# Batch 0 of a linear-attention and feed-forward kernel: k's sums, denominators, division and turns in another order

## The chip, the cores and the metric

The kernel runs on one core of a Trainium2 chip. The core has five engines that run side by side, each through its own instructions in order: TensorE (PE in the profile; PEld is its loading of weights), VectorE (DVE), ScalarE (ACT), GpSimd (POOL) and SyncE (SP). They wait for one another by semaphores. Data comes from the chip's memory by DMA, which SyncE and GpSimd issue here. The metric is the device time of one execution in microseconds (us).

## The reference

```python
theta = np.pi / 2.0 * pos / S                      # S = 576 positions
phi(x) = concat([relu(x) * cos(theta), relu(x) * sin(theta)])   # 64 -> 128 features
q_p, k_p = phi(q), phi(k)                          # 8 batches, 8 heads
kv  = einsum('bhsf,bhsd->bhfd', k_p, v)
z   = sum(k_p, axis=2)                             # the sums of k
num = einsum('bhsf,bhfd->bhsd', q_p, kv)
den = einsum('bhsf,bhf->bhs', q_p, z)[..., None] + 1e-06
x   = (num / den) as [4608 tokens, 512]
h   = x @ w_in                                     # 512 x 2048
out = (h * sigmoid(1.702 * h)) @ w_out             # 2048 x 512
```

Inputs and output are float32; the kernel multiplies in bfloat16 and adds up in float32.

## The kernel before

Work goes batch by batch. Each batch has 576 tokens: four chunks of 128 (0 to 3) and a tail of 64 (chunk 4). The order of every engine's instructions is the order in which the program is written; nothing reorders it. A helper layer puts in the semaphore waits from the tiles that instructions read and write, and hands out buffers from pools: `pmm` has four one-bank PSUM tiles named `mm`, `pat` has two two-bank PSUM tiles named `at`.

For batch 0 nothing can hide the attention, so it stands alone at the start of the program (from `idle(22)`, line 377, to `start_block(0)`, line 416):

- SyncE loads k and then q in two pieces each. GpSimd waits for the first piece of k (the copy into `gate`, L137) and then issues v in two halves that are cast to bfloat16 on the way (`vb`, L139), then the three pieces of w_in, then the loads of batch 1: `load(kf, k, 1)` (line 419), two pieces of w_out, `load_q(1)` (line 422), v, two more pieces of w_out. A load waits until the steps that read its target tile before are done, and holds up what is behind it in GpSimd's queue.
- `idle` (L340) gives TensorE matmuls of zeros while k is on its way.
- `trig` (L151 on ScalarE, L153 on VectorE) makes one of nine steps j of relu times cosine or sine, 64 positions each and all heads, of k (into `kr`) or of q (into `qn0`).
- `kv_mm` (L214) multiplies k's features with a right-hand side, for head pair i, step j and each head of the pair in its own half of the partitions (64 rows), adding up over j. With a column of ones it gives k's sums z (column 64 of the `at` tile), later with `vb` the 64 columns of kv. `kv_evac` (L219) copies 65 columns a head to `kvs` in bfloat16.
- `qturn_pe` (L182) turns two steps of q (a chunk c) by TensorE, `qevac` (L190 on ScalarE, L192 on VectorE) copies the turned q into `qT`.
- `num_mm(c)` (L227) multiplies chunk c of qT with kvs: 64 numerators and one denominator a head. `num_div(c)` adds 1e-6 to the eight denominators (L235), takes reciprocals (L237) and multiplies (L239) into `xn`.
- `xturn_mm(c)` (L256) turns xn into the unused columns of the same `at` tile, `xturn_evac` (L263) copies it with ScalarE into `xT`, the left input of the feed-forward part.
- `start_block` (line 348): `mm1_part` (L279) makes the first four output blocks of x times w_in a chunk of tokens at a time, with the chunks' products and turns in between; `gelu` (L284) is ScalarE's activation into `g`; `mm1` is a whole block of 512 tokens.

Then come the other blocks of mm1, the tail's (L300), and `mm2` (L328), the product of g with w_out, whose result ScalarE copies (L332) and GpSimd stores (L335). Within mm2 of batch 0 stands the attention of batch 1 (lines 425 to 463: its k steps, q steps with DMA transposes, products, divisions and turns), the handover; the program then calls `start_block(1, opened=True)`. From there on batches repeat in a loop (line 466), with the next batch's attention hidden in the same way.

Of the kernel before, what the change touches and what calls it, by code (L numbers as in the profile page):

```python
# [19 lines left out]
def kernel(  # L20
# [64 lines left out]
    ones = const.tile([128, 2], BF16)  # L85
    nc.vector.memset(ones, 1.0)
# [59 lines left out]
    def trig(dst, src, j, act=False):  # L146
        i = src[:, :, ts(j, 64)]
        for cs, w in enumerate((cosw, sinw)):
            o = dst[:, j, :, ts(cs, 64)]
            if act:  # L150
                nc.scalar.activation(o, i, AF.Relu, scale=w[:, j:j + 1])  # L151
            else:
                nc.vector.tensor_scalar(o, i, 0.0, w[:, j:j + 1], op0=MAX, op1=MUL)  # L153
# [45 lines left out]
    st = {}  # L199

    def kv_open(i0=0, i1=NI):
        t = pat.tile([128, 2, 512], F32, name="at")
        for i in range(i0, i1):
            st["kv", i] = t[:, :, ds((i - i0) * 65, 65)]
        st["ps", i0] = t[:, :, 0:(i1 - i0) * 65]
        if i0 == 0:
            st["kvs"] = small.tile([128, 2, NI, VW], BF16, name="kvs", bufs=2)
# [9 lines left out]
    def kv_evac(i0, i1):  # L217
        o = st["kvs"][:, :, i0:i1, 0:65]
        nc.vector.tensor_copy(o, st["ps", i0].rearrange("p hh (i e) -> p hh i e", e=65))  # L219

    nums = {}

# [8 lines left out]
    def num_div(c):  # L231
        ps = nums[c][0]
        pv = ps[:, :, 0:260].rearrange("p a (h e) -> p a h e", h=4)
        den = small.tile([128, 2, 4], F32, name="den")
        nc.vector.tensor_scalar(den, pv[:, :, :, 64], 1e-6, None, op0=ADD)  # L235
        inv = small.tile([128, 2, 4], F32, name="inv")
        nc.vector.reciprocal(inv, den)  # L237
        xn = small.tile([128, 2, 4, 64], BF16, name="xn", bufs=4)
        nc.vector.tensor_tensor(xn, pv[:, :, :, 0:64],  # L239
                                inv.unsqueeze(3).to_broadcast([128, 2, 4, 64]), op=MUL)  # L240
        nums[c].append(xn)
# [9 lines left out]
    def xturn_mm(c):  # L251
        ps, xn = nums[c]
        xv = xn.rearrange("p a h e -> p (a h e)")
        for kc in range(KC):
            o = ps[:, kc // 2, ds(264 + (kc % 2) * 64, 64)].bitcast(BF16)
            nc.tensor.transpose(o, xv[:, ts(kc, 128)], ident)  # L256

    def xturn_evac(b, c):
        ps = nums.pop(c)[0]
# [3 lines left out]
        nc.scalar.activation(o, i, AF.Copy)  # L263
# [84 lines left out]
    def start_block(b, opened=False):  # L348

        if not opened:  # L350
            xturn_mm(0)
            xturn_evac(b, 0)
            xturn_mm(1)
            xturn_evac(b, 1)
            num_mm(2)
            num_div(2)
# [20 lines left out]
    idle(22)  # L377
    for j in (0, 1):
        trig(kr, kf, j)
    for j in (2, 6, 7, 8):  # L380
        trig(kr, kf, j, act=True)
    for j in (3, 4, 5):
        trig(kr, kf, j)
    kv_open(0, 2)
    kv_open(2, 4)
    kv_mm(0, NI, lambda r, i, j: ones[r, 0:1], 64, 1)
    for j in (0, 1):
        trig(qn0, qf0, j)
    qturn_pe(0)
    for j in (2, 3):  # L390
        trig(qn0, qf0, j, act=True)
    qturn_pe(1)
    idle(3)
    for j in (4, 5):
        trig(qn0, qf0, j)
    qturn_pe(2)
    for j in (6, 7):
        trig(qn0, qf0, j, act=True)
    qevac(0)
    trig(qn0, qf0, 8)  # L400
    qevac(1, act=True)
    qevac(2, act=True)
    kv_mm(0, 2, vb_rhs, 0, 64)
    kv_evac(0, 2)
    kv_mm(2, 4, vb_rhs, 0, 64)
    kv_evac(2, 4)
    qturn_pe(3)
    qevac(3, act=True)
    num_mm(0)
    num_div(0)  # L410
    num_mm(1)
    num_div(1)
    qturn_pe(4)
    qevac(4)
    x_open(0)
    start_block(0)
# [11 lines left out]
    for fc in range(5, FC):  # L428
        mm1(0, fc)
# [17 lines left out]
    mm2(0, 3, 8, 12)  # L447
    num_mm(0)
# [4 lines left out]
    mm2(0, 0, 12, 16)  # L453
    mm2(0, 1, 12, 16)
    xturn_mm(0)
    xturn_evac(1, 0)
    mm2(0, 2, 12, 16)
# [5 lines left out]
    start_block(1, opened=True)  # L463
# [79 lines left out]
```

## Time and profile before

| what | value |
|---|---|
| median of 3 runs | 292.15 us (292.04 to 292.19) |
| the profiled execution's own time | 292.69 us |
| its span | 291.0 us |
| TensorE busy | 282.5 us, 97% |
| VectorE busy | 123.9 us, 43% |
| ScalarE busy | 128.6 us, 44% |
| chain that ended last: line 328 (mm2) and line 279 (mm1) | 43% and 36% of the span |
| chain: load of v's first batch | 3% |

The profile is of one execution; times in it count from the start of its span. A group line gives the source line, the engine, the operation, output and inputs, the shapes and how often it ran. A line of the view in order of time gives start, length, engine, line and operation, and in brackets how long the engine had been idle and who released it. The ends of matmuls are modelled: a record of TensorE runs on some 0.2 us after the next one could start, so starts are the better measure of its pace.

### The profile page before, as it was taken

Reading aid. Unit: us, or ns where it says so; the run is one execution under the profiler, and the core shown is the slowest. Engines: PE = TensorE matmul, PEld = TensorE weight load, DVE = VectorE, ACT = ScalarE, POOL = GpSimd, SP = SyncE. Lnnn points to the kernel's source line nnn. Section 1 sums busy time; section 2 is a strip of 40 time slices with the busy share of each in tenths; the row PEclk is TensorE's granted clock in tenths of the full one; section 3 lists DMA queues with packets and bytes.
Section 4 is the critical chain, followed back from the end, with each engine's and each line's share of the span. In section 5 each row is a group of like instructions: output and inputs, shape, how many; then the busy total and the mean of one; then the engine's idle time right before and its main releaser. Section 6 shows DMA issues by size and latency. Waiting matters only on the chain.

```text
span 291.0 us, 5997 instructions
## 1 busy us (share of the span) xinstructions
PE 282.5 (97%) x2427; PEld 157.7 (54%) x2461; DVE 123.9 (43%) x355; ACT 128.6 (44%) x224; POOL 52.9 (18%) x60
## 2 busy tenths in 40 slices
PE   8979999999999999999999999999999999999995
PEld 3775646857545555555545554555455545565444
DVE  4774514872369036912692259415950520000000
ACT  7948633673115621463046313641265116773111
POOL 6250002200216100610143013401150010000000
PEclk9999999999999999999999999999999999999999
DMA  7999998998999885999598948995760341000322
GB/s 247 244 221 288 345 174 207 366 240 208 380 192 201 251 298 136 151 242 335 145 155 225 355 128 151 188 345 159 153 147 0 79 112 38 1 0 8 86 88 72
DMA packets 73211, 53.54 MB, mean 184 GB/s; under 512 B 52608, under 2 KB 62592, under 8 KB 73184
## 3 DMA queue, kind: packets, MB, share of 16 engines
q1 hardware_dynamic: 67216, 37.24, 53.4%
q0 software_dynamic: 5968, 15.93, 20.3%
q8 instruction: 19, 0.31, 0.4%
q14 instruction: 8, 0.07, 0.1%
HBM read 36.70 MB, written 9.44 MB: 159 GB/s over the span
## 4 chain that ended last, share of the span: by engine, by line
PE 91%; DMA 4%; ACT 1%; DVE 1%; issue 1%; POOL 0%; ACTq 0%
PE mm L328 43%; PE mm L279 36%; PE mm L307 4%; PE at L227 3%; PE at L214 3%; DMA vb<-in_v_dram 3%; PE mm L300 2%; ACT g L284 1%; DMA kf<-in_k_dram 1%; PE at L256 1%; DVE xn L239 1%; POOL vb L139 0%; DVE inv L237 0%; PE mm L182 0%; DVE den L235 0%
## 5 line engine op out<-in xcount | busy, mean ns | idle before, releaser
L328 PE MATMUL mm<-w_out_sb,g 128*128 128x512 bf16 (+1 forms) x507 | 116.0, 373 | 1.2 <-issue 0.2
L279 PE MATMUL mm<-xT,w_in 128*128 128x512 bf16 (+1 forms) x598 | 112.7, 345 | 0.5
L284 ACT ACTIVATE g<-mm 128x512 bf16<-128x512 f32 x128 | 75.6, 598 | 32.0 <-PE mm L279 31.9
L279 PEld LDWEIGHTS <-w_in 128*128 128x128 bf16 x608 | 61.7, 113 | 49.1
L328 PEld LDWEIGHTS <-g 128*128 128x128 bf16 x528 | 48.8, 98 | 50.0
L335 POOL DMA_DIRECT2D out_dram<-ysb x34 | 42.0, 1236 | 174.9 <-ACT ysb L332 174.8
L332 ACT ACTIVATE ysb<-mm 128x512 f32<-128x512 f32 (+1 forms) x37 | 21.7, 586 | 115.8 <-PE mm L328 115.8
L219 DVE CAST kvs<-at 128x520 bf16<-128x520 f32 (+1 forms) x9 | 5.8, 642 | 55.7 <-PE at L214 55.7
L239 DVE TENSOR_TENSOR xn<-at,inv 128x512 bf16<-128x512 f32 x40 | 27.7, 692 | 2.0 <-DMA xT<-xn 0.7
L153 DVE TENSOR_SCALAR kr<-kf,cosw 128x256 bf16<-128x256 f32 x68 | 23.9, 352 | 9.5 <-DMA kf<-in_k_dram 9.5
L153 DVE TENSOR_SCALAR kr<-kf,sinw 128x256 bf16<-128x256 f32 x68 | 23.2, 341 | 0.0
L235 DVE TENSOR_SCALAR den<-at 128x8 f32<-128x8 f32 x40 | 6.6, 166 | 37.1 <-PE at L227 37.1
L227 PEld LDWEIGHTS <-qT 128*128 128x128 bf16 x320 | 14.5, 97 | 7.3
L166 DVE TENSOR_SCALAR qn<-qf,cosw 128x512 bf16<-128x512 f32 (+1 forms) x33 | 15.8, 479 | 3.4 <-DMA qf<-in_q_dram 3.4
L227 PE MATMUL at<-kvs,qT 128*128 128x65 bf16 x320 | 15.9, 193 | 0.0
L166 DVE TENSOR_SCALAR qn<-qf,sinw 128x512 bf16<-128x512 f32 (+1 forms) x33 | 15.8, 479 | 0.0
L328 PE MATMUL mm<-w_out_sb,gt 128*128 128x512 bf16 x62 | 13.9, 380 | 0.2 <-issue 0.2
L214 PEld LDWEIGHTS <-kr 64*128 64x128 bf16 x648 | 10.2, 94 | 3.7 <-issue 3.0
L307 PE MATMUL mm<-xt,w_in 128*128 128x384 bf16 x64 | 10.6, 326 | 0.0
L328 PEld LDWEIGHTS <-gt 128*128 128x128 bf16 x64 | 6.2, 98 | 7.3
L174 DVE CAST vt<-vf 128x2304 bf16<-128x2304 f32 (+1 forms) x7 | 8.9, 1266 | 0.7 <-DMA vf<-in_v_dram 0.7
L307 PEld LDWEIGHTS <-w_in 128*128 128x128 bf16 x64 | 7.2, 113 | 3.3
(57 smaller groups left out, 101.9 us busy)
## 6 DMA issues: line engine op xcount, KB each, us to landing
kf<-in_k_dram SPq DMA_DIRECT2D x6, 1152.0 KB, 9.6
vf<-in_v_dram SPq DMA_DIRECT2D x6, 1152.0 KB, 12.4
qf<-in_q_dram SPq DMA_DIRECT2D x6, 1024.0 KB, 7.2
out_dram<-ysb POOLq DMA_DIRECT2D x24, 256.0 KB, 2.9
w_out_sb<-in_moe_w_out_dram POOLq DMA_DIRECT2D x4, 512.0 KB, 17.4
out_dram<-ysb POOLq DMA_DIRECT2D x10, 128.0 KB, 7.5
kf<-in_k_dram POOLq DMA_DIRECT2D x1, 1152.0 KB, 12.2
vf<-in_v_dram POOLq DMA_DIRECT2D x1, 1152.0 KB, 20.1
```

The lines of the kernel that those rows point to most:

```text
L153: nc.vector.tensor_scalar(o, i, 0.0, w[:, j:j + 1], op0=MAX, op1=MUL)
L166: nc.vector.tensor_scalar(o, i, 0.0, sc, op0=MAX, op1=MUL)
L174: nc.vector.tensor_copy(o, i)
L214: nc.tensor.matmul(st["kv", i][:, hh, ds(col, n)], kr[r, j, i, :], rhs(r, i, j), start=(j == 0), stop=(j == NS - 1))
L227: nc.tensor.matmul(ps[:, h // 4, ds((h % 4) * 65, 65)], qT[:, h, ts(c, 128)], st["kvs"][:, hh, i, 0:65], start=True, stop=True)
L239: nc.vector.tensor_tensor(xn, pv[:, :, :, 0:64], inv.unsqueeze(3).to_broadcast([128, 2, 4, 64]), op=MUL)
L279: nc.tensor.matmul(hp[fc][:, t0:t1], wcol(kc, fc), x[b][:, kc, t0:t1], start=(kc == 0), stop=(kc == KC - 1))
L284: nc.scalar.activation(g, hp.pop(fc), AF.Gelu_apprx_sigmoid)
L307: nc.tensor.matmul(hps[:, 128:B * 64], wcol(kc, fc), xt[:, kc, 128:B * 64], start=(kc == 0), stop=(kc == KC - 1))
L328: nc.tensor.matmul(yp[b, t, c0][:, c0:c1], w, w_out_sb[:, fc, c0:c1], start=(fc == 0), stop=(fc == FC - 1))
L332: nc.scalar.activation(ysb[:, c0:c1], yp[b, t, c0][:, c0:c1], AF.Identity)
L335: eng.dma_start(out=dst[:, c0:c1], in_=ysb[p0:p0 + n, c0:c1])
```

## The change

In batch 0:

- k's sums come from a new function `ksum`, with both heads of a pair in one matmul: all 128 rows of k's features against a selector `sel` of two columns (ones for the upper half of the partitions in one column, for the lower half in the other). 36 matmuls take the place of 72. They go into an `mm` tile, and VectorE copies the eight sums into column 64 of `kvs`. The kv products then have 64 columns a head and no longer share a tile with the sums (`kv_open` and `kv_evac` get a width n).
- The denominators of chunks 0 and 1 come from a new function `den_mm` (eight matmuls of one column, qT against the sums), with the addition and the reciprocal in `inverse`, both ahead of the product with v. For the other chunks `num_div` calls `inverse` itself, as before.
- The division of chunks 0 and 1 is made in two halves of four heads (`halves=True`), and their turns and ScalarE's copies in halves of two turns (`xturn_halves`).
- q's chunks 0 to 3 are all turned ahead of the product with v; q's copies stand in another order, and q's last step (j=8) and chunk 4 (turn, product, division) move behind the first parts of mm1.
- One of k's eight ScalarE steps (cosine of j=6) goes to VectorE.
- The 22 idle matmuls of 512 columns become 94 of 64 columns and 6 of 512; the three later ones become two.
- mm1's blocks 5 and 6 are called inside batch 0's script, between chunk 4's steps; the loop after it starts at 7.

In the handover from batch 0 to batch 1, `mm2(0, 0, 12, 16)` moves ahead of the first two products, and `mm2(0, 2, 12, 16)` is cut into two pieces around the first turns. `start_block` loses the part for batch 0 and is now used for batch 1 alone.

```diff
@@ -82,8 +82,11 @@
     scale = math.pi / 2.0 / S
     halfpi = const.tile([128, 1], F32)
     nc.vector.memset(halfpi, math.pi / 2.0)
-    ones = const.tile([128, 2], BF16)
-    nc.vector.memset(ones, 1.0)
+
+    sel = const.tile([128, 2], BF16)
+    nc.vector.memset(sel, 0.0)
+    nc.vector.memset(sel[0:64, 0:1], 1.0)
+    nc.vector.memset(sel[64:128, 1:2], 1.0)
     nc.scalar.activation(sinw, pos_f, AF.Sin, scale=scale)
     nc.scalar.activation(cosw, pos_f, AF.Sin, scale=-scale, bias=halfpi)
     gl = const.tile([128, 1], F32)
@@ -144,10 +147,11 @@
 
 
     def trig(dst, src, j, act=False):
+
         i = src[:, :, ts(j, 64)]
         for cs, w in enumerate((cosw, sinw)):
             o = dst[:, j, :, ts(cs, 64)]
-            if act:
+            if act is True or (act == "sin" and cs == 1):
                 nc.scalar.activation(o, i, AF.Relu, scale=w[:, j:j + 1])
             else:
                 nc.vector.tensor_scalar(o, i, 0.0, w[:, j:j + 1], op0=MAX, op1=MUL)
@@ -198,11 +202,11 @@
 
     st = {}
 
-    def kv_open(i0=0, i1=NI):
+    def kv_open(i0=0, i1=NI, n=65):
         t = pat.tile([128, 2, 512], F32, name="at")
         for i in range(i0, i1):
-            st["kv", i] = t[:, :, ds((i - i0) * 65, 65)]
-        st["ps", i0] = t[:, :, 0:(i1 - i0) * 65]
+            st["kv", i] = t[:, :, ds((i - i0) * n, n)]
+        st["ps", i0] = t[:, :, 0:(i1 - i0) * n]
         if i0 == 0:
             st["kvs"] = small.tile([128, 2, NI, VW], BF16, name="kvs", bufs=2)
 
@@ -214,11 +218,38 @@
                     nc.tensor.matmul(st["kv", i][:, hh, ds(col, n)], kr[r, j, i, :], rhs(r, i, j),
                                      start=(j == 0), stop=(j == NS - 1))
 
-    def kv_evac(i0, i1):
-        o = st["kvs"][:, :, i0:i1, 0:65]
-        nc.vector.tensor_copy(o, st["ps", i0].rearrange("p hh (i e) -> p hh i e", e=65))
+    def kv_evac(i0, i1, n=65):
+        o = st["kvs"][:, :, i0:i1, 0:n]
+        nc.vector.tensor_copy(o, st["ps", i0].rearrange("p hh (i e) -> p hh i e", e=n))
+
+    def ksum():
+
+        t = pmm.tile([128, 512], F32, name="mm")
+        for i in range(NI):
+            for j in range(NS):
+                nc.tensor.matmul(t[:, ts(i, 2)], kr[:, j, i, :], sel,
+                                 start=(j == 0), stop=(j == NS - 1))
+        nc.vector.tensor_copy(st["kvs"][:, :, :, 64].rearrange("p hh i -> p i hh"),
+                              t[:, 0:8].rearrange("p (i hh) -> p i hh", hh=2))
 
     nums = {}
+
+    inv_of = {}
+
+    def inverse(c, sums):
+        den = small.tile([128, 2, 4], F32, name="den")
+        nc.vector.tensor_scalar(den, sums, 1e-6, None, op0=ADD)
+        inv_of[c] = small.tile([128, 2, 4], F32, name="inv")
+        nc.vector.reciprocal(inv_of[c], den)
+
+    def den_mm(c):
+
+        ps = pmm.tile([128, 512], F32, name="mm")
+        for h in range(H):
+            i, hh = divmod(h, 2)
+            nc.tensor.matmul(ps[:, h:h + 1], qT[:, h, ts(c, 128)], st["kvs"][:, hh, i, 64:65],
+                             start=True, stop=True)
+        return ps[:, 0:8].rearrange("p (a h) -> p a h", a=2)
 
     def num_mm(c):
         ps = pat.tile([128, 2, 512], F32, name="at")
@@ -228,16 +259,15 @@
                              st["kvs"][:, hh, i, 0:65], start=True, stop=True)
         nums[c] = [ps]
 
-    def num_div(c):
+    def num_div(c, halves=False):
         ps = nums[c][0]
         pv = ps[:, :, 0:260].rearrange("p a (h e) -> p a h e", h=4)
-        den = small.tile([128, 2, 4], F32, name="den")
-        nc.vector.tensor_scalar(den, pv[:, :, :, 64], 1e-6, None, op0=ADD)
-        inv = small.tile([128, 2, 4], F32, name="inv")
-        nc.vector.reciprocal(inv, den)
+        if c not in inv_of:
+            inverse(c, pv[:, :, :, 64])
+        inv = inv_of.pop(c).unsqueeze(3).to_broadcast([128, 2, 4, 64])
         xn = small.tile([128, 2, 4, 64], BF16, name="xn", bufs=4)
-        nc.vector.tensor_tensor(xn, pv[:, :, :, 0:64],
-                                inv.unsqueeze(3).to_broadcast([128, 2, 4, 64]), op=MUL)
+        for a in (slice(0, 1), slice(1, 2)) if halves else (slice(0, 2),):
+            nc.vector.tensor_tensor(xn[:, a], pv[:, a, :, 0:64], inv[:, a], op=MUL)
         nums[c].append(xn)
 
     x = {}
@@ -248,19 +278,26 @@
     def x_cols(b, c):
         return x[b][:, :, ts(c, 128)] if c < 4 else xt[:, :, ts(b, 64)]
 
-    def xturn_mm(c):
+    def xturn_mm(c, kcs=range(4)):
         ps, xn = nums[c]
         xv = xn.rearrange("p a h e -> p (a h e)")
-        for kc in range(KC):
+        for kc in kcs:
             o = ps[:, kc // 2, ds(264 + (kc % 2) * 64, 64)].bitcast(BF16)
             nc.tensor.transpose(o, xv[:, ts(kc, 128)], ident)
 
-    def xturn_evac(b, c):
-        ps = nums.pop(c)[0]
+    def xturn_evac(b, c, a0=0, a1=2):
+        ps = nums[c][0]
         n = 128 if c < 4 else 64
         i = ps[:, :, 264:392].bitcast(BF16).rearrange("p a (k t) -> p a k t", k=2)[:, :, :, 0:n]
         o = x_cols(b, c).rearrange("p (a k) t -> p a k t", a=2)
-        nc.scalar.activation(o, i, AF.Copy)
+        nc.scalar.activation(o[:, a0:a1], i[:, a0:a1], AF.Copy)
+        if a1 == 2:
+            nums.pop(c)
+
+    def xturn_halves(b, c):
+        for a in range(2):
+            xturn_mm(c, (2 * a, 2 * a + 1))
+            xturn_evac(b, c, a, a + 1)
 
     def xturn_dma(b, c):
         xn = nums.pop(c)[1]
@@ -345,15 +382,8 @@
     def vt_rhs(r, i, j):
         return vt[r, j, i, 0:65]
 
-    def start_block(b, opened=False):
-
-        if not opened:
-            xturn_mm(0)
-            xturn_evac(b, 0)
-            xturn_mm(1)
-            xturn_evac(b, 1)
-            num_mm(2)
-            num_div(2)
+    def start_block(b):
+
         for c in range(4):
             for fc in range(4):
                 mm1_part(b, fc, c * 128, c * 128 + 128)
@@ -374,46 +404,79 @@
         xturn_evac(b, 4)
 
 
-    idle(22)
+    idle(94, 64)
+    idle(6)
     for j in (0, 1):
         trig(kr, kf, j)
-    for j in (2, 6, 7, 8):
-        trig(kr, kf, j, act=True)
+    trig(kr, kf, 2, act=True)
     for j in (3, 4, 5):
         trig(kr, kf, j)
-    kv_open(0, 2)
-    kv_open(2, 4)
-    kv_mm(0, NI, lambda r, i, j: ones[r, 0:1], 64, 1)
+    trig(kr, kf, 6, act="sin")
+    for j in (7, 8):
+        trig(kr, kf, j, act=True)
+    kv_open(0, 2, 64)
+    kv_open(2, 4, 64)
     for j in (0, 1):
         trig(qn0, qf0, j)
-    qturn_pe(0)
     for j in (2, 3):
         trig(qn0, qf0, j, act=True)
+    ksum()
+    qturn_pe(0)
+    qevac(0)
     qturn_pe(1)
-    idle(3)
+    dens = [den_mm(0)]
+    idle(2)
     for j in (4, 5):
         trig(qn0, qf0, j)
-    qturn_pe(2)
     for j in (6, 7):
         trig(qn0, qf0, j, act=True)
-    qevac(0)
-    trig(qn0, qf0, 8)
-    qevac(1, act=True)
+    inverse(0, dens[0])
+    qevac(1)
+    qturn_pe(2)
     qevac(2, act=True)
-    kv_mm(0, 2, vb_rhs, 0, 64)
-    kv_evac(0, 2)
-    kv_mm(2, 4, vb_rhs, 0, 64)
-    kv_evac(2, 4)
     qturn_pe(3)
     qevac(3, act=True)
+    kv_mm(0, 2, vb_rhs, 0, 64)
+    kv_evac(0, 2, 64)
+    inverse(1, den_mm(1))
+    kv_mm(2, 4, vb_rhs, 0, 64)
+    kv_evac(2, 4, 64)
     num_mm(0)
-    num_div(0)
+    num_div(0, halves=True)
     num_mm(1)
-    num_div(1)
+    num_div(1, halves=True)
+    x_open(0)
+    xturn_halves(0, 0)
+    xturn_halves(0, 1)
+    num_mm(2)
+    num_div(2)
+
+    def x_part(c):
+        for fc in range(4):
+            mm1_part(0, fc, c * 128, c * 128 + 128)
+
+    x_part(0)
+    num_mm(3)
+    num_div(3)
+    xturn_mm(2)
+    xturn_evac(0, 2)
+    x_part(1)
+    xturn_mm(3)
+    xturn_evac(0, 3)
+    trig(qn0, qf0, 8)
+    x_part(2)
+    x_part(3)
+    for fc in range(4):
+        gelu(fc)
+    mm1(0, 4)
     qturn_pe(4)
     qevac(4)
-    x_open(0)
-    start_block(0)
+    mm1(0, 5)
+    num_mm(4)
+    num_div(4)
+    mm1(0, 6)
+    xturn_mm(4)
+    xturn_evac(0, 4)
 
 
     load(kf, k, 1)
@@ -425,7 +488,7 @@
     load_wout(3)
     for j in range(NS):
         trig(kr, kf, j)
-    for fc in range(5, FC):
+    for fc in range(7, FC):
         mm1(0, fc)
     mm1_tail_first(0, 0)
     mm1_tail_first(0, 1)
@@ -445,22 +508,23 @@
     kv_evac(0, 4)
     mm2(0, 2, 8, 12)
     mm2(0, 3, 8, 12)
+    mm2(0, 0, 12, 16)
     num_mm(0)
     num_div(0)
     num_mm(1)
     num_div(1)
     x_open(1)
-    mm2(0, 0, 12, 16)
     mm2(0, 1, 12, 16)
+    mm2(0, 2, 12, 14)
     xturn_mm(0)
     xturn_evac(1, 0)
-    mm2(0, 2, 12, 16)
+    mm2(0, 2, 14, 16)
     xturn_mm(1)
     xturn_evac(1, 1)
     num_mm(2)
     num_div(2)
     mm2(0, 3, 12, 16)
-    start_block(1, opened=True)
+    start_block(1)
 
 
     for b in range(1, B):
```

## The prediction

> **What bounds the kernel now.** I read the page first, then TensorE's waits, then the stretches by window, then the order of time from 8 to 24 us, and last the handover to batch 1 near 47 us.
>
> ```profile
> PE 282.5 (97%) x2427; PEld 157.7 (54%) x2461; DVE 123.9 (43%) x355; ACT 128.6 (44%) x224; POOL 52.9 (18%) x60
> ```
>
> TensorE is busy for 97% of the span, so only time in which it has nothing to do can be won. Where it waits, the view of its waits says:
>
> ```profile
> PE at L256 <- DVE xn L239: 1.4, 2, 0.8
> PE at L214 <- DMA vb<-in_v_dram: 0.4, 1, 0.4
> PE mm L328 <- issue: 0.3, 2, 0.2
> ```
>
> All of it but 0.3 us lies in batch 0's attention. The windows (TensorE's busy time is the first figure after the length; the last three are granted clock, DMA share, GB/s) put it between 12.4 and 17.1 us; after that TensorE is full, so a shift of the first x by some time shifts the end by as much:
>
> ```profile
> 12.40:14.00 1.60, 1.16 (x49) 1.05 (x45) 0.79 (x2) 1.28 (x2) 1.09 (x3) 1.00 1.23 207
> 14.00:17.10 3.10, 1.71 (x38) 1.36 (x36) 2.43 (x8) 1.62 (x3) 3.10 (x5) 1.00 1.23 207
> 17.10:23.20 6.10, 5.95 (x103) 5.35 (x101) 3.18 (x9) 3.55 (x7) 1.45 (x3) 1.00 1.11 265
> 23.20:43.50 20.30, 20.20 (x149) 10.90 (x148) 8.05 (x25) 12.29 (x21) 0.55 (x1) 1.00 1.15 262
> ```
>
> The chain in order of time (start, length, what):
>
> ```profile
> 11.12 0.69 DVE L192 COPY qT<-mm 128x1024 bf16<-128x1024 bf16 x1
> 11.72 0.35 DVE L153 TENSOR_SCALAR qn<-qf,cosw 128x256 bf16<-128x256 f32 x1
> ...
> 12.89 0.71 PE L214 MATMUL at<-vb,kr 64*128 64x64 bf16 x36 [0.44 <-DMA vb<-in_v_dram]
> ...
> 13.54 0.62 PE L182 MATMUL mm<-ident,qn 128*128 128x128 bf16 x8
> 13.64 0.43 DVE L219 CAST kvs<-at 128x260 bf16<-128x260 f32 x1 [0.71 <-PE at L214]
> ...
> 14.44 0.17 DVE L235 TENSOR_SCALAR den<-at 128x8 f32<-128x8 f32 x1 [0.37 <-PE at L227]
> ...
> 14.88 0.69 DVE L239 TENSOR_TENSOR xn<-at,inv 128x512 bf16<-128x512 f32 x1
> 15.49 0.15 DVE L235 TENSOR_SCALAR den<-at 128x8 f32<-128x8 f32 x1
> ...
> 15.63 0.40 PE L256 MATMUL at<-ident,xn 128*128 128x128 bf16 x4 [0.76 <-DVE xn L239]
> ...
> 16.06 0.60 ACT L263 ACTIVATE xT<-at 128x512 bf16<-128x512 bf16 x1 [0.85 <-PE at L256]
> ...
> 17.14 1.06 PE L279 MATMUL mm<-xT,w_in 128*128 128x128 bf16 x16
> ```
>
> The second half of v lands, TensorE multiplies, VectorE copies and divides, TensorE turns, ScalarE copies, and the first product with w_in starts at 17.14. Records of TensorE include a tail of some 0.2 us; from start to start, 8 turns take 0.46 (13.54 to 13.99), 4 turns 0.23, 8 products of 65 columns 0.24, 16 products of 128 columns 0.90, a half of kT v 0.65 (12.89 to 13.54).
>
> **The change part by part.** Times are on this trace's axis.
>
> Sums of k. VectorE now does one step of k more (its cos of j=6), so its last ends at 8.60 (7.99 + 0.26 + 0.35), where ScalarE ended at 8.67. 30 of the 36 new matmuls remain then. No row shows a full 128-row load with 2 columns: the old ones go at 14 ns (56 in 0.79), the 65-column products at 30. I take 28, twice the half-height load, so 0.84, done at 9.5; bounds 14 and 60 ns move it by -0.4 and +1.0, and only what passes 9.8 counts, so 0 to +0.7 us. The small copy of the sums runs beside the turns.
>
> q's turns. VectorE's four steps of chunk 0 end at 9.76; chunk 0's second half of turns starts at 9.81 and ends at 10.21 (0.40). The copy to qT (0.69) now stands **ahead** of steps j=4, 5 on VectorE, which before ran while q landed (10.07 to 11.21). They now run 10.84 to 11.99 (0.60 after the copy's start, as 11.12 to 11.72 shows, then 3 x 0.265 + 0.35). Behind them TensorE has half of chunk 2 (12.04 to 12.27) and chunk 3 (to 12.73), both now ahead of v in its queue. So kT v's first half starts at 12.73, not 11.75; the two chunks' denominators (8 one-column products, 0.24) follow, and the second half starts at 13.70, not 12.89: v is no longer what it waits for. **+0.81**. The reciprocals and chunk 1's copy on VectorE end by 13.04, beside this.
>
> Division and turns. From the second half's start to the copy of kvs is 0.75 and from the copy's end to VectorE's first look at the product 0.37, as before: 14.45, 14.88, 15.25. The den and reciprocal (0.44, from 14.44 to 14.88) are gone from the chain, for two chunks. The halves: 256 elements a division, which I price at 0.42 by the 0.43 of the 260-element copy (0.35 from one half of 0.69) with 0.35 from start to start. But the built program carries two waits that the diff does not show: the first half's turns wait for **both** divisions of their chunk, and the second half's turns wait until ScalarE has **copied out the first half**. So: divisions end at 16.02; turns 16.07 (two take 0.29 to their end); copy 16.39 to 16.82 (0.43, the row of 256 elements of xt); turns 16.87; copy 17.19 to 17.62; chunk 1's first half beside that, copy 17.52 to 17.95; its last turns 18.00 to 18.12; and behind them in TensorE's queue the third chunk's product (0.24) and x's first part: 18.36 instead of 17.14. **+1.22**, the 0.81 included.
>
> From there to x's last part. Before, 17.14 to 21.02 (3.88): two products of 65 columns, two sets of turns, three parts of 0.90, a wait of 0.25 for xn at 18.53. Now chunk 4's product is gone from it, the wait is nearly the same (0.24; xn is ready 1.38 after its product's last start, as 14.24 to 15.62 before): 3.65. **-0.23**.
>
> After it. Chunk 4's turn of q (0.23) and product (0.24) are now in TensorE's full stretch, where before the first filled an idle spot. Its x turns stand one mm1 (0.86) behind its product, and xn needs 1.38: a new wait of 0.52. **+0.99**. That mm1(5) and mm1(6) go ahead of the turns costs nothing itself; they are only taken out of the later loop.
>
> Handover. One mm2 group of four (0.86) moves ahead of the products, which leaves 0.86 + 0.43 + 0.23 + 0.43 = 1.95 between chunk 1's last product and its turns; xn of chunk 1 is ready 2.66 after the first product's start (46.45 to 49.06, + 0.05), and TensorE comes there at 0.48 + 1.95 = 2.43. **+0.23**; before there was none. Bounds 0 to 0.3.
>
> What else moves. q's last step (j=8) goes behind xn of chunk 3 on VectorE, to about 21. GpSimd's load of the next q waits for it, so it is issued near 21.5 instead of 15.58, and the next v and the last two loads of w_out are queued behind it. I take 0, since DMA share is above 1 in both windows from 17.1 to 43.5: the backlog of k, w_in and w_out covers the gap. The worst is the whole 5.9 us less the 2.0 by which TensorE is later and the 0.86 of the moved group, 3.0. The next batch's k steps start behind one more division (25.99 becomes some 26.9); their user is at 43.5. ScalarE has four copies of 0.43 for two of 0.60 and idles at L263 anyway.
>
> The idle matmuls. 22 wide ones took 7.10, the first eleven at 0.43. Narrow ones cost at least 1/8 of that, 53 ns, at most some 60 (twice the 30 of 65 columns), so 94 and 6 end near 7.5, ahead of k at 8.6: 0.
>
> Sum: 1.22 - 0.23 + 0.99 + 0.23 = **+2.21 us**. The profiled execution took 292.69 (span 291.0 and 1.69 around it), so 294.9; it stands 0.54 above the median 292.15, so **294.35** as a median.
>
> **The rivals.**
> A. The clock. TensorE ran its first 4.4 us at half pace and was granted 1.00 since, though busy only 1.71 of 3.10 us from 14.0 to 17.1. From 7.5 on it now gets mostly thin work. If full pace came one period later, sums and turns would run 0.8 longer: 295.1; if it fell again before 13.9, the 2.6 us of TensorE's work on the chain would double: 296.9. The quoted stretch, which kept 1.00, speaks against it. The Trainium skill (TensorE: Matmul & The Clock Gate, Parts 1 and 4) says that an idle window brings the half clock back and that transposes don't count as busy; by that rule this change runs the risk. The 14.0 to 17.1 row, full of transposes, shows no drop.
> B. The halves overlap after all, because the two added waits cost nothing. Then x starts at 17.14, and the sum is -0.23 + 0.99 + 0.23: 293.1. The waits in the program speak against it.
> C. Not slower: v stays what TensorE waits for, because q's side on VectorE is done by 12.9. It decides if kT v's second half starts by 12.9; together with B that takes 0.81 more: 292.3, no measurable change. Against it: VectorE's line of 9.76, 10.93, 11.99 has no gap to give.
> D. The late q load reaches the handover: up to 297.3.
>
> **How the numbers follow.** My forecast 0.77, of its own range 293.6 to 295.3 (the sums' +0.7, the handover's and divisions' bounds); A 0.07, B 0.07, C 0.05, D 0.04. From 293.0 to 296.2 it leaves out C and parts of A and D and the tails of the first, under 2 in 10. A measurement tells 0.2%, 0.58 us, from nothing: C is the same (0.05) or a little faster; a gain needs C and the later waits gone as well, 0.04; slower is the rest.
>
> **What would show it.** In the changed trace: kT v's second half starts 13.4 to 14 with VectorE's q steps ahead of it, not v's DMA; ScalarE's four half copies of xT alternate with pairs of turns, 0.8 apart; x's first part starts near 18.4; TensorE waits 0.5 for xn one mm1 after chunk 4's product, and 0.2 for it in the handover; from there both traces run in parallel, 2.2 apart. Wrong would be: v's DMA still named before kT v, pairs of turns back to back, or a granted clock under 1.00 after 6 us.

## The result and the profile after

The changed kernel takes 296.53 us in the median of six executions (294.87 to 297.26); before it was 292.14. The ratio is 1.0145, with a 95% interval of 1.0114 to 1.0177: slower. The prediction said slower, but 294.35, and its range ended at 296.2, so it was wrong by its size.

The spread is the first thing to read, since in these executions the kernel before spreads over 0.15 us and this one over 2.4. The six executions fall into three groups by the mean clock that TensorE was granted: 1.000 (294.87), 0.993 (295.81, 295.85), 0.987 to 0.988 (297.21 to 297.26). The median lies between the second group and the third, where no execution was. The profiled execution took 295.85 (span 294.1, mean clock 0.993) and belongs to the middle group. From the page of the changed kernel, the busy time of the engines and the clock in forty slices:

```profile
PE 286.5 (97%) x2518; PEld 162.3 (55%) x2518; DVE 124.6 (42%) x362; ACT 127.9 (43%) x224; POOL 52.1 (18%) x60
PEclk9979999999999999999999999999999999999999
```

The span is 3.1 us longer, and one slice, the third (14.7 to 22.1 us), has a lower clock. The windows of the same execution (length, busy time and count of each engine, then granted clock, DMA share, GB/s) put its ends on 16.85 and 20.27 us:

```profile
13.44:16.85 3.41, 2.04 (x66) 1.72 (x65) 2.54 (x8) 1.29 (x2) 2.37 (x4) 1.00 1.25 211
16.85:20.27 3.42, 2.89 (x33) 2.72 (x33) 1.06 (x3) 1.04 (x3) 0.00 (x0) 0.50 1.12 209
20.27:23.68 3.41, 3.30 (x62) 3.15 (x61) 1.58 (x5) 1.49 (x3) 0.82 (x1) 1.00 1.08 341
```

The half clock lasts 3.41 us. It lies on the last turns and the first products with w_in, which are work that nothing hides. It also begins a whole number of such lengths, three, behind the point where the trace's record of the full clock starts (6.62), which is why the windows here are cut in this way.

In order of time the changed kernel's chain reads (cuts marked by dots):

```profile
10.18 0.69 DVE L196 COPY qT<-mm 128x1024 bf16<-128x1024 bf16 x1 [0.39 <-PE mm L186]
10.79 0.34 DVE L157 TENSOR_SCALAR qn<-qf,cosw 128x256 bf16<-128x256 f32 x1
...
12.75 0.70 PE L218 MATMUL at<-vb,kr 64*128 64x64 bf16 x36
...
13.67 0.70 PE L218 MATMUL at<-vb,kr 64*128 64x64 bf16 x36
...
15.21 1.41 DVE L270 TENSOR_TENSOR xn<-at,inv 128x256 bf16<-128x256 f32 x4 [0.37 <-PE at L258]
...
16.02 0.27 PE L286 MATMUL at<-ident,xn 128*128 128x128 bf16 x2 [0.60 <-DVE xn L270]
...
16.32 0.38 ACT L293 ACTIVATE xT<-at 128x256 bf16<-128x256 bf16 x1 [1.98 <-DVE xn L270]
16.76 0.52 PE L286 MATMUL at<-ident,xn 128*128 128x128 bf16 x4 [0.47 <-ACT xT L293]
...
17.11 0.66 ACT L293 ACTIVATE xT<-at 128x256 bf16<-128x256 bf16 x2 [0.40 <-PE at L286]
17.82 0.37 PE L286 MATMUL at<-ident,xn 128*128 128x128 bf16 x2 [0.53 <-ACT xT L293]
...
18.44 1.90 PE L316 MATMUL mm<-xT,w_in 128*128 128x128 bf16 x16
```

v's load is named nowhere: q's steps j=4, 5 start 0.61 behind the start of the copy to qT, and the product with v comes when TensorE gets to it: v's second half had landed by 13.10, where GpSimd's copy that waits for it starts, and is first used at 13.67. The turns run in pairs, each held by ScalarE's copy of the pair before it. The sixteen first products take 1.90 instead of 1.06, because they run at half clock. The waits of TensorE in the changed kernel (total, times, longest) say the same, with new ones for the copies:

```profile
...
PE at L286 <- ACT xT L293: 1.0, 2, 0.5
PE at L286 <- DVE xn L270: 1.0, 2, 0.6
PE mm L230 <- DVE kr L157: 0.4, 2, 0.2
PE at L258 <- DVE kvs L223: 0.3, 1, 0.3
...
```

Where the 3.1 us between the two profiled executions lie follows from the starts of the same work in both traces. The first product with w_in: 17.14 and 18.44, +1.30. The tail products of batch 0: 32.67 and 35.61, +2.94. x's last parts in the handover: 54.04 and 57.19, +3.15. The tails at the end: 253.15 and 256.30, +3.15. So all of it arises in batch 0's attention and the handover, and the steady loop adds nothing.

### The profile page after: what moved, and what is told of

Same layout as the page of the kernel before. It is cut to its first block, busy times and chain, and to the rows that moved or that the text cites. A ratio compares the mean times of both kernels' runs of the same rounds, so it can differ in the third digit from the quotient of the medians.

```text
span 294.1 us, 6155 instructions
## 1 busy us (share of the span) xinstructions
PE 286.5 (97%) x2518; PEld 162.3 (55%) x2518; DVE 124.6 (42%) x362; ACT 127.9 (43%) x224; POOL 52.1 (18%) x60
## 4 chain that ended last, share of the span: by engine, by line
PE 93%; DVE 2%; DMA 2%; issue 1%; ACT 0%; SPq 0%; ACTq 0%
PE mm L365 42%; PE mm L316 37%; PE mm L344 4%; PE at L218 3%; PE at L258 3%; DMA qf<-in_q_dram 2%; PE mm L337 1%; DVE xn L270 1%; PE at L286 1%; PE mm L186 1%; DVE qn L157 0%; DVE inv L243 0%; ACT xT L293 0%; DVE qT L196 0%; PE mm L250 0%
## 5 line engine op out<-in xcount | busy, mean ns | idle before, releaser
L365 PE MATMUL mm<-w_out_sb,g 128*128 128x512 bf16 (+1 forms) x528 | 117.4, 372 | 0.0
L316 PE MATMUL mm<-xT,w_in 128*128 128x512 bf16 (+1 forms) x608 | 114.7, 348 | 0.0
L372 POOL DMA_DIRECT2D out_dram<-ysb x34 | 41.1, 1210 | 176.6 <-ACT ysb L369 176.5
L270 DVE TENSOR_TENSOR xn<-at,inv 128x512 bf16<-128x512 f32 (+1 forms) x42 | 27.7, 665 | 1.7 <-PE at L258 0.4
L218 PEld LDWEIGHTS <-kr 64*128 64x128 bf16 x576 | 9.1, 94 | 2.6 <-issue 2.5
```

Source lines behind the costliest of these rows:

```text
L218: nc.tensor.matmul(st["kv", i][:, hh, ds(col, n)], kr[r, j, i, :], rhs(r, i, j), start=(j == 0), stop=(j == NS - 1))
L270: nc.vector.tensor_tensor(xn[:, a], pv[:, a, :, 0:64], inv[:, a], op=MUL)
L316: nc.tensor.matmul(hp[fc][:, t0:t1], wcol(kc, fc), x[b][:, kc, t0:t1], start=(kc == 0), stop=(kc == KC - 1))
L365: nc.tensor.matmul(yp[b, t, c0][:, c0:c1], w, w_out_sb[:, fc, c0:c1], start=(fc == 0), stop=(fc == FC - 1))
L372: eng.dma_start(out=dst[:, c0:c1], in_=ysb[p0:p0 + n, c0:c1])
```

## The experiments

Each was timed beside the kernel before, in four groups on four chips; the changed kernel itself was timed in the first comparison alone and not beside its variants. Since a fall of TensorE's clock is a thing that some executions have and others don't, two numbers are given: the median of the executions without such a fall (mean clock 0.997 or more), with what it is above the kernel before of the same comparison, also without falls; and how many executions had one. The kernel before had one in 5 of its 69 executions in these comparisons. The changed kernel itself: 294.87, 2.73 above, with a fall in 5 of 6, 3 of them two (by the mean clock, which is as far below 1 again; no such execution was profiled).

| kernel | full clock | above before | falls | ratio, 95% interval |
|---|---|---|---|---|
| changed | 294.87 | 2.73 | 5 of 6 | 1.0145, 1.0114 to 1.0177 |
| changed, later stretch filled | 294.83 | 2.73 | 2 of 4 | 1.0102, 1.0069 to 1.0135 |
| changed, both stretches filled | 294.85 | 2.62 | 0 of 4 | 1.0089, 1.0074 to 1.0104 |
| changed, wide idle matmuls | 294.73 | 2.63 | 3 of 4 | 1.0139, 1.0076 to 1.0202 |
| changed, whole division and turns | 294.06 | 1.96 | 0 of 6 | 1.0058, 1.0040 to 1.0076 |
| ... and chunk 4's turns later | 293.54 | 1.31 | 2 of 4 | 1.0071, 1.0052 to 1.0091 |
| ... or q's chunk 3 behind v | 293.40 | 1.15 | 1 of 7 | 1.0043, 1.0026 to 1.0059 |
| ... or v later | 294.12 | 1.89 | 2 of 4 | 1.0083, 1.0062 to 1.0105 |
| changed, all of these undone | 292.73 | 0.60 | 0 of 12 | 1.0011, 0.9999 to 1.0024 |
| before, halved division and turns | 292.86 | 0.76 | 4 of 10 | 1.0040, 1.0021 to 1.0059 |
| before, new handover | 292.39 | 0.14 | 0 of 12 | 1.0001, 0.9989 to 1.0014 |
| before, v later | 292.32 | 0.09 | 1 of 10 | 1.0001, 0.9987 to 1.0015 |
| before, chunk 4's turns first | 291.84 | -0.41 | 1 of 12 | 0.9988, 0.9976 to 1.0000 |

The intervals are of all executions, falls included; a difference of 0.1 to 0.2 us between rows is not to be read, and the full-clock figure of the changed kernel is a single execution, that with wide idle matmuls too.

**The later thin stretch filled.** Theory 1 was that the clock fell because TensorE had too little to do between 14.3 and 17.1.

```diff
     def xturn_halves(b, c):
         for a in range(2):
+            idle((3, 2, 0, 3)[2 * c + a])
             xturn_mm(c, (2 * a, 2 * a + 1))
             xturn_evac(b, c, a, a + 1)
...
     def idle(n, cols=512):
+        if n == 0:
+            return
```

> The changed kernel with eight more idle matmuls of 512 columns where TensorE waits for batch 0's division and copies (three ahead of the first pair of turns, two ahead of the second, three ahead of the fourth: 0.65, 0.43 and 0.65 us of waits of 0.7, 0.6 and 0.8). Theory 1, the clock: what my sum of +2.2 us lacks is the half clock that begins near 17 us, because TensorE's work between 14.3 and 17.1 is too thin. Then the granted clock is 1.00 in every execution, the sixteen first products take 0.90 from start to start instead of 1.68, and the time is about 294.9 with little spread, 1.6 us less than the changed kernel's median of 296.5. Theory 2, the spread and the rest come from elsewhere (transfers, the late q load): time and spread stay, 294.9 to 297.3. Theory 3: idle matmuls only get in the way: slower than 296.5.

The four took 294.74 and 294.92 at clocks of 0.998 and 1.000, and 295.91 and 295.95 at 0.994. Two falls in one execution did not come again, but single ones did. In the profiled execution the fall is elsewhere now; its windows:

```profile
7.31:10.72 3.41, 2.16 (x48) 1.85 (x48) 3.11 (x10) 2.58 (x7) 0.28 (x1) 1.00 1.16 280
10.72:14.14 3.42, 2.91 (x33) 2.06 (x36) 1.97 (x7) 2.62 (x6) 0.90 (x3) 0.50 1.23 205
14.14:17.55 3.41, 3.07 (x101) 2.37 (x99) 2.20 (x8) 1.02 (x2) 1.81 (x3) 1.00 1.22 210
```

The filled stretch is kept at full clock, and the half clock follows another one: k's sums with their two columns, q's turns and the wait for the first copy to qT. The theory was half right, as there are two thin stretches. The filling itself costs nothing: the full-clock time is that of the changed kernel.

**Whole division and turns.**

```diff
-    num_div(0, halves=True)
+    num_div(0)
     num_mm(1)
-    num_div(1, halves=True)
+    num_div(1)
     x_open(0)
-    xturn_halves(0, 0)
-    xturn_halves(0, 1)
+    xturn_mm(0)
+    xturn_evac(0, 0)
+    xturn_mm(1)
+    xturn_evac(0, 1)
```

> The changed kernel with division, turns and copies of chunks 0 and 1 whole again, everything else as changed. Theory 1: the halves cost 1.1 us on the chain (copy of the first half between the two pairs of turns, twice), so the first product with w_in starts at 17.3 instead of 18.44, and since the thin stretch is that much shorter, the clock falls less often: 293.7 where it stays 1.00, 294.7 to 296 where it falls. Rival: the halves overlap well enough, and undoing them changes nothing at a clock of 1.00 (294.9).

294.06, with all six at a clock of 1.000. TensorE in order of time:

```profile
13.54 0.70 PE L218 MATMUL at<-vb,kr 64*128 64x64 bf16 x36
...
15.82 0.40 PE L286 MATMUL at<-ident,xn 128*128 128x128 bf16 x4 [0.54 <-DVE xn L270]
16.42 0.40 PE L286 MATMUL at<-ident,xn 128*128 128x128 bf16 x4 [0.20 <-DVE xn L270]
16.91 0.40 PE L258 MATMUL at<-kvs,qT 128*128 128x65 bf16 x8
17.14 1.06 PE L316 MATMUL mm<-xT,w_in 128*128 128x128 bf16 x16
```

From the second half of the product with v to the first product with w_in it is 3.60 us. So undoing the halves wins 0.8 at full clock, and with no fall in these six, 2.5 against the changed kernel's median. The falls are rarer without the halves and not gone: the three variants of this kernel below had them in 2 of 4, 2 of 4 and 1 of 7. The 1.1 that I expected at full clock was too much by 0.3, and the rival, that they overlap, is out.

**The wide idle matmuls of before.**

```diff
-    idle(94, 64)
-    idle(6)
+    idle(22)
```

> The changed kernel with the 22 wide idle matmuls of before in place of 94 narrow and 6 wide. Theory 1: the narrow ones are not what lets the clock fall at 17 us; k's sums start at the same 8.2 to 8.6, and the clock still falls near 17 us in most executions: 294.9 to 297.3 as with the change. Rival: the narrow ones leave the clock's governor with too little work, and with the wide ones the clock is 1.00 throughout: 294.9.

294.73, 295.93, 296.32 and 298.30, the last three with falls: no change that four executions can tell. In its profile the clock falls at 18.73, after a stretch from 15.32 in which TensorE was busy 1.70 of 3.41 us. So the narrow idle matmuls are not what brings the falls. The 298.30, by its clock (0.988) an execution with two falls, is 3.6 above the one without; in the changed kernel two cost 2.4.

**The halves alone, in the kernel before.**

```diff
...
-        nc.vector.tensor_tensor(xn, pv[:, :, :, 0:64],
-                                inv.unsqueeze(3).to_broadcast([128, 2, 4, 64]), op=MUL)
+        inv = inv.unsqueeze(3).to_broadcast([128, 2, 4, 64])
+        for a in (slice(0, 1), slice(1, 2)) if halves else (slice(0, 2),):
+            nc.vector.tensor_tensor(xn[:, a], pv[:, a, :, 0:64], inv[:, a], op=MUL)
...
-            xturn_mm(0)
-            xturn_evac(b, 0)
-            xturn_mm(1)
-            xturn_evac(b, 1)
+            xturn_halves(b, 0)
+            xturn_halves(b, 1)
...
-    num_div(0)
+    num_div(0, halves=True)
     num_mm(1)
-    num_div(1)
+    num_div(1, halves=True)
```

> The kernel before with the halved division, turns and copies of chunks 0 and 1 alone. Theory 1: the first product with w_in starts 0.8 us later (17.9 instead of 17.14), as the pairs of turns alternate with ScalarE's copies: 292.9 to 293.0 at full clock; the thin stretch from 14.5 grows to 3.4 us, so a fall of the clock, with 1 us or more on top, is possible here. Rival: the halves overlap, 291.8.

0.76 more at full clock (expected 0.8), and 4 of 10 executions at 0.994 with 294.1 to 294.4. One part of the change alone thus brings both effects: the longer chain, and the fall of the clock in four in ten where the kernel before has it in 5 of 69 (1 of 15 beside it). TensorE's order shows the same alternation as in the changed kernel:

```profile
15.08 0.27 PE L257 MATMUL at<-ident,xn 128*128 128x128 bf16 x2 [0.82 <-DVE xn L241]
15.83 0.63 PE L257 MATMUL at<-ident,xn 128*128 128x128 bf16 x4 [0.47 <-ACT xT L264]
16.93 0.27 PE L257 MATMUL at<-ident,xn 128*128 128x128 bf16 x2 [0.47 <-ACT xT L264]
```

**Both thin stretches filled.**

```diff
     idle(94, 64)
-    idle(6)
+    idle(9)
...
     qturn_pe(1)
+    idle(2)
     dens = [den_mm(0)]
...
         for a in range(2):
+            idle((3, 2, 0, 3)[2 * c + a])
```

> The changed kernel with idle matmuls in both thin stretches: those of the first filled kernel (14.3 to 18 us), and five more between 7.9 and 11.5, three behind the first idle matmuls and two ahead of chunk 0's denominators. Theory 1, the clock: with only the later stretch filled, the two falls of the clock (297.2) did not come again, but one fall did (295.9), and in the profile it began at 11.0, behind the stretch of two-column sums and turns. With both filled the clock is 1.000 in every execution and the time 294.7 to 295.0. Rival: the governor doesn't go by such gaps, and 295.9 stays in about half of the executions.

294.53, 294.78, 294.91 and 295.23, none with a fall. The windows of its profile, cut at the same length from where its record of the full clock starts (4.34):

```profile
7.75:11.17 3.42, 2.67 (x58) 2.27 (x60) 2.80 (x11) 2.26 (x7) 0.00 (x0) 1.00 1.18 259
11.17:14.58 3.41, 3.15 (x95) 2.20 (x93) 2.52 (x10) 3.41 (x6) 1.29 (x3) 1.00 1.23 205
14.58:17.99 3.41, 3.02 (x48) 1.82 (x41) 1.97 (x6) 0.96 (x4) 1.43 (x3) 1.00 1.21 212
```

Same chain, 13 more idle matmuls, 1.7 us less in the median. Four executions are few, but the changed kernel went without a fall in one of six, and two other variants on the same chip fell in 2 of 4 each.

**Chunk 4's turns one block later** (on the kernel with whole division and turns).

```diff
     mm1(0, 6)
+    mm1(0, 7)
     xturn_mm(4)
...
-    for fc in range(7, FC):
+    for fc in range(8, FC):
```

> The changed kernel with whole division and turns in chunks 0 and 1 (294.06, clock 1.000 throughout), and chunk 4's x turns one block of mm1 later, so that mm1(7) stands ahead of them too. Theory: the wait of 0.5 us for chunk 4's xn, which the prediction prices at 0.52, is gone: 293.5. Rival: ScalarE's activations or the PSUM tiles hold TensorE there instead, and the time stays 294.06.

293.44 and 293.64 at full clock, 294.65 and 294.73 with a fall. The wait is gone, and the rival with it; 0.52 less in the time itself, 0.65 by the distance to the kernel before.

**v later, in the kernel before and in the one with whole division and turns.** The same edit in both:

```diff
     nc.gpsimd.tensor_copy(gate[0:1, 0:1], kf[0:1, 0, 0:1])
+    late = const.tile([128, 512], BF16)
+    nc.gpsimd.memset(late, 0.0)
+    nc.gpsimd.tensor_copy(gate[0:1, 2:3], late[0:1, 0:1])
```

> The kernel before with some 0.7 us of GpSimd work (a memset of 512 columns and a dependent copy) ahead of the load of v. Theory 4: before, the landing of v's second half lies on the chain, and the profiled execution stood 0.54 above the median because v landed that much later in it; so 0.7 us more show as 0.5 to 0.7: 292.6 to 292.8. Rival: v has slack in an ordinary execution, and the time stays 292.1.

> The changed kernel with whole division and turns in chunks 0 and 1 (294.06), and the same 0.7 us ahead of the load of v. Theory 4: with q's turns ahead of it in TensorE's queue the product with v starts near 12.6 and 13.5, later than v lands, so the delay is hidden: 294.0 to 294.2. Rival: v is still on the chain, 294.6 to 294.8.

The second came as expected: 294.07 and 294.17 at full clock against 294.06. The first didn't: 292.32 against 292.23, nothing that can be measured. The pair is a weak test, though. The edit moves the issue of v from some 4.4 to 5.1, but v's landing (the start of GpSimd's copy that waits for it) differs from execution to execution by more: 12.55 and 12.84 in the two profiles with the edit, anything from 12.09 to 13.29 in the twelve without it.

What settles v are the traces. In the profiled execution of before, v's second half landed at 12.91, and from the first half's start to the turns behind the second half it is 1.79 us (11.75 to 13.54). In the profile of the kernel with the new handover, whose batch 0 is that of before, v landed at 12.11 and both halves go in one piece (order of time, TensorE):

```profile
11.85 1.24 PE L214 MATMUL at<-vb,kr 64*128 64x64 bf16 x72
13.02 0.62 PE L182 MATMUL mm<-ident,qn 128*128 128x128 bf16 x8
```

1.17 us from 11.85 to 13.02, so v held the profiled execution of before up by 0.62, and that execution stood 0.55 above the median. This one stood at its median (292.40 and 292.39). The kernel with chunk 4's turns first has the same batch 0 up to there, and in its profile v is later still:

```profile
11.86 0.71 PE L214 MATMUL at<-vb,kr 64*128 64x64 bf16 x36
13.16 0.71 PE L214 MATMUL at<-vb,kr 64*128 64x64 bf16 x36 [0.59 <-DMA vb<-in_v_dram]
13.80 0.62 PE L182 MATMUL mm<-ident,qn 128*128 128x128 bf16 x8
```

There it is 1.94 us, 0.77 more, and that execution (292.65) stands 0.81 above its kernel's full-clock median of 291.84. So with this batch 0, v is late in some executions and is paid for, and has slack in others. In the changed kernel the second half starts at 13.67, behind every landing seen here.

**The new handover alone, in the kernel before.**

```diff
     mm2(0, 3, 8, 12)
+    mm2(0, 0, 12, 16)
     num_mm(0)
...
-    mm2(0, 0, 12, 16)
     mm2(0, 1, 12, 16)
+    mm2(0, 2, 12, 14)
     xturn_mm(0)
     xturn_evac(1, 0)
-    mm2(0, 2, 12, 16)
+    mm2(0, 2, 14, 16)
```

> The kernel before with the changed handover from batch 0 to batch 1 alone (one mm2 group moved ahead of the products, one cut in two). Theory: chunk 1's turns then come 0.2 us before their xn is ready, 292.3 against 292.1; in the changed kernel's trace the whole handover took 0.21 more. Rival: it fills a wait that the trace doesn't show, and the time is 291.9 or less.

292.39 against 292.25; the ratio's interval holds 1, so the time can't tell. The traces can: from the tail products of batch 0 to x's last parts it is 21.37 us in before (32.67 to 54.04), 21.59 in this kernel (32.16 to 53.75) and 21.58 in the changed one (35.61 to 57.19).

**Chunk 4's turns ahead of mm1(4), in the kernel before.**

```diff
-        mm1(b, 4)
         xturn_mm(4)
+        mm1(b, 4)
         xturn_evac(b, 4)
```

> The kernel before with the turns of chunk 4 of batches 0 and 1 ahead of mm1(4) instead of behind it. There TensorE waits 0.15 to 0.2 us for the first activation to give its PSUM tile back, and chunk 4's xn has been ready for 0.7 us: the turns (0.23) fill that wait in both batches. Theory: 0.3 us less, 291.8. Rival: the copy of the turns delays nothing but the wait only moves to the next block, 292.1.

291.84 at full clock, 0.41 less than before; the ratio over all executions is 0.9988 (0.9976 to 1.0000). It is the one version here that is ahead of both kernels, by 0.1%, at the edge of what can be told.

**q's chunk 3 behind the product with v again** (on the kernel with whole division and turns).

```diff
-    qturn_pe(3)
-    qevac(3, act=True)
     kv_mm(0, 2, vb_rhs, 0, 64)
...
     kv_evac(2, 4, 64)
+    qturn_pe(3)
+    qevac(3, act=True)
```

> The changed kernel with whole division and turns in chunks 0 and 1 (294.06 at full clock), and q's chunk 3 turned behind the product with v again, as before. Theory: the product with v starts 0.46 earlier and its second half 0.3 to 0.4 earlier (chunk 1's denominators then wait for their q), and the turn hides behind the copy of kvs: 293.6 to 293.8 at full clock. Rival: v's landing takes over and nothing is won, 294.0. Falls of the clock, as in other kernels of this kind, may add 1.1 us to some executions.

293.40 at full clock (293.6 to 293.8 were expected), 0.65 less than with chunk 3 ahead of v (0.81 by the distance to the kernel before). Its trace shows 0.45 of that: from chunk 2's turns to the first product with w_in it is 5.25 us (11.65 to 16.90) instead of 5.70 (11.44 to 17.14). The rest is not explained, and sizes of 0.2 us are at the edge of what a few executions tell.

**All of it undone.** The four edits to the changed kernel together (whole division and turns, chunk 3 behind v, chunk 4's turns one block later, the handover as before), and `idle(9)` and `idle(2)` in the first thin stretch (a part of the edit):

```diff
-    idle(6)
+    idle(9)
...
+    idle(2)
     dens = [den_mm(0)]
...
-    num_div(0, halves=True)
+    num_div(0)
...
-    mm2(0, 0, 12, 16)
     num_mm(0)
```

> The changed kernel with every step undone that an experiment or the traces priced: whole division and turns (0.81 less), q's chunk 3 behind the product with v (0.65 less), chunk 4's x turns one more block of mm1 later (0.52 less), the handover as before (0.2 less), and five idle matmuls of 512 columns in the first thin stretch. k's sums by the selector, the early denominators, the order of chunk 4's q turn and the narrow idle matmuls stay. Theory: 294.87 less 2.18, so 292.7 at full clock, and the clock falls in few executions or none; what is left against 292.25 is chunk 4's q turn and product in TensorE's full stretch (0.47). Rival: the prices overlap, and 293.2 or more remains; or the sums and denominators cost something themselves.

292.73 at full clock, and no fall in twelve executions; the ratio is 1.0011 (0.9999 to 1.0024). The prices add up: 2.14 less than 294.87, where the sum of the single prices is 2.18. What remains of the change (the sums by the selector, the early denominators, chunk 4's q turn in the full stretch) is 0.60 above before at full clock, where 0.47 were expected: no gain shows in it.

## Why the prediction was wrong, step by step

**k's sums: right.** The 30 matmuls took 0.75 from start to start (8.55 to 9.30), 25 ns each where I took 28, and the second half of chunk 0's turns waited for q, not for them.

**q's turns: right.** VectorE's copy ahead of j=4, 5, and the product with v at 12.75 and 13.67 where the sum has 12.73 and 13.70. v is no longer waited for. That 13.70 fits is luck: the working's own terms (12.73, half of kT v 0.65, denominators 0.24) make 13.62, and the denominators took 0.29. Also, the eight products between the halves are the denominators of chunk 1 alone; those of chunk 0 stand ahead of v.

**Division and turns: the mechanism right; that 18.36 in the sum and 18.44 in the trace lie so close is luck.** The two waits that the program carries are there: `ACT xT L293` ends TensorE's idle time twice. Chunk 2's product started 0.14 earlier than in the sum (17.98 instead of 18.12); at half clock (from 16.85 on) it then took 0.46 instead of 0.24, so that the first product with w_in came 0.08 late. As a part by itself the halves cost 0.76 to 0.81, with the rival B (293.1) out.

**From there to x's last part: the step that failed.** The sum has 3.65 us; the trace has 4.52 (18.44 to the last part at 22.06 + 0.90). The difference of 0.87 is the half clock: 0.79 on the sixteen first products (1.69 from start to start instead of 0.90) and 0.08 on the product of 65 columns behind them, in which the clock rises again. The sum took every duration on TensorE from rows at full clock and gave the clock no term; with the 0.22 of the step before, the fall took some 1.1 us in this trace. In the kernel with whole division and turns, without a fall, the same step is 3.66 (17.14 to 20.80), as the sum has it.

**After it: right.** A wait of 0.5 us one mm1 behind chunk 4's product; the shift from x's last part to mm1(7) is 4.88 (22.96 to 27.84), where the 3.88 of before (21.02 to 24.90) and the 0.99 of the sum make 4.87.

**Handover: right in the traces**, +0.21 and +0.22 for +0.23; too small for the time alone to show.

**What else moves: right.** GpSimd issued the load of the next q at 22.86 instead of 15.58, and it landed at the same time all the same: VectorE's first step, which waits for it in both traces, starts at 34.19, before at 34.18. Rival D did not happen.

**From the profiled execution to the median: wrong, by 0.54.** The sum gives 294.90 on the axis of the profiled execution, and 294.87 is what the changed kernel took in its one execution at full clock. The fit to 0.03 is better than the sum deserves, since the same chain with idle matmuls in it took 294.53 to 295.23 at full clock. But I then took off the 0.54 by which the profiled execution stood above the median of before. Those 0.54 were v, late in that one execution, and the chain of before waits for v. The changed kernel doesn't (v landed at 13.10 and was first needed at 13.67), so it had nothing to give back. I had the row for it (TensorE's 0.4 us wait for v) and had said myself that v is no longer what TensorE waits for.

**Rival A: right in kind, wrong in place and chance.** I gave it 0.07 and the clock fell in five of six executions. I had it on k's sums and the turns of q, by a late rise or a fall before 13.9; in the changed kernel's profile it came at 16.85, behind the halved division and turns, and doubled the first products with w_in, for which I had no price. A granted clock under 1.00 after 6 us was one of the signs that the prediction named. (In two variants, the filled one and the one with v later, it did come earlier, at 10.72 and 11.64.) That the costs, 0.96 above 294.87 for one fall and 2.4 for two, lie inside the rival's 0.8 to 2.6 is therefore in part luck. What misled me was reading one quiet stretch of one execution of before as proof. Its stretch from 14.0 to 17.1 kept the full clock at 1.71 us of work in 3.10, but whether a thin stretch is followed by half clock differs from execution to execution of the same kernel: before, the clock fell in 5 of 69. The change made TensorE's work thinner in two places (two-column sums and a wait for q's copy from 8 to 11.5, pairs of turns with waits from 14.3 to 18).

In all four profiles with a fall it begins a whole number of 3.41 us behind the first rise (two, two, three and four), and the rise itself comes anywhere from 3.90 to 7.14 us, though TensorE starts at 1.25 or 1.26 in each. So the same thin stretch can lie inside one such period or across the edge of two, as that of before did, cut at 15.94. The Trainium skill's rule in TensorE: Matmul & The Clock Gate, Part 1, that the window is free-running and so the same kernel meets it at another phase each time, agrees with these numbers. The idle window that the prediction cites from the Trainium skill there is not what stands ahead of the falls: TensorE's longest wait in the changed kernel's period was 0.6 us. That page also counts transposes as not busy (Part 4); no run here separates transposes from other thin work.

So of the 4.4 us to the median, 2.2 are the sum's own steps, 0.54 is the wrong conversion, and 1.66 (296.53 less 294.87) is the clock: the median of six executions of which two had one fall and three had two.

What is shown is that filling TensorE's waits takes the falls away (0 of 4 with both stretches filled, 0 of 12 in the last kernel, which fills one and shortens the other) and that the halves alone bring them into the kernel before (4 of 10). What stays open is the quantity that decides a fall. Busy time alone doesn't: the periods of 3.41 us ahead of the four falls seen in profiles had TensorE busy for 2.04, 2.16, 1.70 and 2.48 us, and periods without a fall had 2.01 (chunk 4's turns first, from 14.90), 2.02 (new handover, from 13.50) and 2.38 (whole division and turns, from 13.04).

## What to carry to other kernels

A sum made against one profiled execution holds on that execution's axis; before it is moved to the median, ask what made that execution differ, and whether the changed kernel still has that in its chain. Where a change replaces dense work on TensorE by waits and one-column products ahead of the main stretch, price half a clock for one period (3.41 us here) right behind it and give it a real chance; idle matmuls in the waits cost nothing here at full clock, and no execution with both stretches filled had a fall. A division or copy cut in halves gains only where the program lets the second half go before the first is copied out: read the waits that the built program carries, since two halves of one PSUM tile were ordered here one after the other.

## What the runs showed of the hardware that was not expected

TensorE's clock fell to half for 3.41 us right at the start of batch 0's dense work in most executions of a kernel whose TensorE, once k was there, had no idle time above 0.6 us in the profile, so no long idle time is needed. One fall cost 0.9 to 1.6 us of device time, two 2.4 to 3.6. And the number of columns did not set the pace of narrow matmuls: 30 products of two columns with full loads of 128 rows started 25 ns apart, 8 denominators of one column at some 27 ns, though their columns differ by a factor of two; the one-column products of before, on 64 rows, went at 14 ns.
